# One sixth of the score subtraction through ScalarE and GpSimd, three slot-softmax operations from GpSimd to VectorE, and the row-max selector product in fp32r

## The chip, the cores and the metric

The kernel runs on one core of a Trainium2 chip. The metric is the device time of one execution in microseconds (us); before the change it is 1116.34 us, the median of three runs (1116.29 to 1117.21). Each engine works through its own queue in order: TensorE (PE; its weight loads are listed apart as PEld), VectorE (DVE), ScalarE (ACT), GpSimd (POOL), and SyncE (SP), which issues DMAs.

## The reference

Attention over pooled keys, then a soft mixture of experts on its output:

```python
kv_flat = kv_pool.reshape(B, -1, C) @ w_sr          # 4 batches, 768 keys each, C = 128
k = v = kv_flat
s = scale * (q @ k.transpose(0, 2, 1))               # 12288 queries a batch
a = np.exp(s - s.max(-1, keepdims=True))
a /= a.sum(-1, keepdims=True) + 1e-09
x = (a @ v).reshape(B * S, D)
logits = x @ phi                                     # 32 slots
d = softmax of logits over all rows (axis 0)
slot_input = d.T @ x                                 # 8 experts, 4 slots each
slot_out[e] = np.maximum(slot_input[e] @ w1[e], 0.0) @ w2[e]
return softmax of logits over the slots (axis 1) @ slot_out
```

## The kernel before, in words

The 49152 queries are cut into 96 blocks of 512 (index `i`), the 768 keys of a batch into six tiles of 128. Scores stand transposed in PSUM, keys on the partitions and queries along the row, in three PSUM tiles `s_0`, `s_1`, `s_2` of two key tiles each; each exists once, so the scores of the next block can be written only when those of this block have been read. A block goes through these steps:

- `q_hi` (ACT, L462) and `q_lo` (POOL, L466) split the queries into two parts, and `qk` (PE, L476 to L478) makes three products for each key tile: 18 products of 512 columns.
- The maximum over the keys of each query: `rowmax1` (DVE, L483), a transposing reduction, once for each PSUM tile; `rowmax2` (DVE, L493 and L495); `rowmax_pe` (PE, L503), which multiplies with a constant selector matrix `sel` in fp32; `rowmax3` (DVE, L508); and `rowmax4` (DVE, L513), which writes the maximum over all partitions as `mb`.
- `sub` (DVE, L521) subtracts `mb` from the scores in four instructions: key tiles 0 and 1 together, 2, 3, then 4 and 5 together. Three key tiles make one half, `t_0` or `t_1`.
- For each half: `exp_hi` (ACT, L528) writes the exponential `phi` in fp16, `exp_t` (ACT, L532) the same in fp32, and `plo` (POOL, L537) their difference, 128x1536 elements.
- The products with the values, `av_hi` (PE, L554 and L555) and `av_lo` (PE, L562), are made about two blocks later, and `av_evac` (ACT, L572) copies them out.

Four blocks make a group, which goes through the slot softmax with a running maximum. Its steps that matter here: `g1l` (L626) makes the logits `LL`; `g2` (DVE, L631 and L633) takes their maximum; `g2q`, `g2h`, `g2l`, `g3m`, `g3` (L588, L643, L647, L654, L661 to L668) turn that into the new running maximum `mrun`; `g4` (L673 and L678) subtracts it; `g5e` (ACT, L682) takes the exponential; `g5m` (L688 and L690) weights it; `g7m` (PE, L707) adds up the slot inputs. `k_max` (DVE, L718), `k_sub` (L723) and `k_exp` (ACT, L728) belong to the softmax over the slots. In nearly all groups `g1l`, `g4`, `g5m` and `k_sub` run on GpSimd.

The order of the instructions on PE, DVE, ACT and POOL is not the order of the code. A planner (`Plan`) takes every step with an engine, a cost in us, a latency, a priority and what it depends on, plays the four queues through with these costs, and issues the steps in the order that comes out. A step marked `hot` (the chain from L493 to L513) may hold an engine back for it. So a changed cost or engine of one step moves many others, and what was issued next to what has to be read from the built program. A block gets 9.8 us in its table (`PER`).

Of the kernel before, what the change touches and what calls it, by code (L numbers as in the profile page):

```python
# [172 lines left out]
def attention_then_soft_moe(ctx: ExitStack, tc: tile.TileContext, qT, kv0, kvT, w_sr, w_srT, phi, w1, w2, outT):  # L173
# [71 lines left out]
    nc.vector.tensor_copy(sel_bf, sel)
# [59 lines left out]
    def kv_pool(h, c):  # L305
        w = KS[h][1] - KS[h][0]
        v = kvs[h, c]
        if c == 0:
            kvs[h] = sp.tile([P, TH, BQ], F32, tag="t", name=f"pool_{h}", bufs=TBUF).rearrange("p a b -> p (a b)")
        a = kvs[h][:, : 2 * w]  # L310
        if c == 2:
            nc.vector.tensor_tensor(out=a, in0=kvs[h, 0], in1=v, op=ALU.add)
        elif c:
            nc.vector.tensor_tensor(out=a, in0=a, in1=v, op=ALU.add)
# [174 lines left out]
    def rowmax2(i):  # L489
        top = banks[plan.bank][:, 512 - (NQD + 1) * NBK :]  # L490
        pq = PQ[i] = top[:, NBK:]
        r1 = top[:, :NBK]
        nc.vector.tensor_reduce(out=r1, in_=MX[i].rearrange("p t b -> p b t"), axis=X, op=ALU.max)  # L493
# [1 line left out]
        nc.vector.tensor_tensor(  # L495
            out=rq, in0=r1.unsqueeze(1).broadcast_to([P, NQD, NBK]),
            in1=quad.unsqueeze(2).broadcast_to([P, NQD, NBK]), op=ALU.mult,
        )
        MX[i] = rq

    def rowmax_pe(i):
        pqv = PQ.pop(i)
        nc.tensor.matmul(pqv, sel, MX[i].rearrange("p k b -> p (k b)"), start=True, stop=True)  # L503
# [12 lines left out]
    def sub(i, t, n):  # L516
        h, o = divmod(t, TH)
        if o == 0:
            TT_[i, h] = sp.tile([P, TH, BQ], F32, tag="t", name=f"t_{i}_{h}", bufs=TBUF)
# [1 line left out]
        nc.vector.tensor_tensor(  # L521
            out=TT_[i, h][:, o : o + n, :], in0=S[i, t // 2][:, u : u + n, :],
            in1=MX[i].unsqueeze(1).broadcast_to([P, n, BQ]), op=ALU.subtract,
        )
# [278 lines left out]

    pooled[0] = bp.tile([P, NK], F32, tag="pooled", name="pooled_0", bufs=1)
    loaded = []
    for n, which in enumerate(LOADS):
        dep = [] if n < 2 else [ops["pool", 0, 6 * (n - 1) - 2]]
        loaded.append(op("SP", 0.3, 0, 0, dep, lambda which=which: start_kv(which)))
        for h, e0, cnt in which:
            for c in range(e0, e0 + cnt, 2):  # L810
# [442 lines left out]
```

## Time and profile before

| | us |
|---|---|
| time, median of 3 runs | 1116.34 |
| profiled execution, first to last instruction | 1112.9 |
| PE busy | 1044.9 |
| DVE busy | 984.2 |
| POOL busy | 870.5 |
| ACT busy | 829.4 |

The profiled execution has no separate time beside its span of 1112.9 us; the runs lie 3.4 us above it, which is what stands around the first and the last instruction. The granted TensorE clock was full from 60 us to 1020 us.

How to read the rows: a timeline row has its start in us, its duration in us, the engine, the line, the operation, what it writes and what it reads, the shape, how many instructions are merged, and in brackets how long the engine was idle before it and who ended that. A row of a group has the count, the busy time in us, the mean duration in ns, and the idle time before it. Starts are those of the record; neighbouring instructions of one engine overlap by some 0.05 to 0.1 us. Blocks are counted from 0; blocks 36 to 39 are one group, and its logits are made while blocks 38 and 39 pass.

### The profile page before, as it was taken

The page shows a single profiled execution, that of the slowest core. Times are in us where ns is not written, and L with a number is a line of the kernel's source. Part 1 is how long each engine was busy: PE and PEld are TensorE (multiplying, and loading weights), DVE is VectorE, ACT ScalarE, POOL GpSimd, SP SyncE. Part 2 cuts the span into 40 slices and gives each one's busy share as a digit, 9 for nine tenths or more (in the row PEclk, how much of TensorE's full clock was granted, in tenths as well). Part 3 has the DMA queues.
Part 4 walks back from the last instruction along what each step waited for, and adds up shares of the span by engine and source line. Part 5 has one row for each costly group of instructions (what it writes and reads, how often), then busy time and mean ns, then how long its engine had stood idle before and what let it go on. Part 6 is the DMA issues. An engine that isn't in the chain of part 4 may idle for free.

```text
span 1112.9 us, 24732 instructions
## 1 busy us (share of the span) xinstructions
PE 1044.9 (94%) x10198; PEld 893.6 (80%) x10198; DVE 984.2 (88%) x1493; ACT 829.4 (75%) x1029; POOL 870.5 (78%) x503
## 2 busy tenths in 40 slices
PE   3699999999999999999999999999999999997885
PEld 2588888888888888888888888888888888886343
DVE  7889889899889989899888988989989988997894
ACT  1677778778777878778777788688778777875563
POOL 0679898798899889789899989789889889873440
PEclk9899999999999999999999999999999999999975
DMA  9218301111136310120145310120110110113498
GB/s 351 108 31 177 70 16 39 39 58 39 39 60 150 82 35 6 39 87 10 39 102 108 82 39 1 39 95 2 39 39 1 39 39 2 39 39 114 145 406 357
DMA packets 17407, 89.15 MB, mean 80 GB/s; under 512 B 1680, under 2 KB 3984, under 8 KB 11152
## 3 DMA queue, kind: packets, MB, share of 16 engines
q1 hardware_dynamic: 13408, 69.47, 17.0%
q0 software_dynamic: 3312, 17.70, 8.4%
q8 instruction: 81, 1.33, 0.5%
q10 hardware_dynamic: 576, 0.41, 0.1%
q14 instruction: 30, 0.25, 0.1%
HBM read 58.87 MB, written 25.17 MB: 76 GB/s over the span
## 4 chain that ended last, share of the span: by engine, by line
PE 61%; ACT 18%; DVE 15%; issue 3%; POOL 2%; DMA 1%; SPq 0%; DVEq 0%; ACTq 0%
PE m L562 10%; PE m L554 10%; PE m L555 9%; ACT phi L528 8%; PE s L476 8%; PE s L478 7%; PE s L477 7%; ACT t L532 7%; DVE t L521 4%; PE m L503 3%; DVE r L483 3%; PE m L707 2%; PE po L1138 2%; DVE o L1147 2%; DVE mb L513 1%
## 5 line engine op out<-in xcount | busy, mean ns | idle before, releaser
L537 POOL TENSOR_TENSOR plo<-t,phi 128x1536 f16<-128x1536 f32 x190 | 598.8, 3156 | 128.1 <-ACT t L532 127.3
L528 ACT ACTIVATE phi<-t,lnk 128x1536 f16<-128x1536 f32 x192 | 301.5, 1570 | 118.9 <-DVE t L521 118.7
L483 DVE TRANSPOSE_TENSOR_REDUCE r<-s 128x32 f32<-128x1024 f32 x288 | 348.6, 1233 | 29.3 <-PE s L478 25.7
L554 PE MATMUL m<-vhi,phi 128*128 128x161 f16 x2280 | 354.7, 234 | 2.8 <-DVE acc L713 1.4
L555 PE MATMUL m<-vlo,phi 128*128 128x160 f16 x2280 | 353.8, 233 | 0.0
L521 DVE TENSOR_TENSOR t<-s,mb 128x1024 f32<-128x1024 f32 (+1 forms) x384 | 342.8, 949 | 9.3
L532 ACT ACTIVATE t<-t,lnk 128x1536 f32<-128x1536 f32 x192 | 301.5, 1570 | 3.6
L476 PE MATMUL s<-qhi,khi 128*128 128x512 f32 x576 | 239.9, 417 | 6.1 <-DVE t L521 5.8
L554 PEld LDWEIGHTS <-phi 128*128 128x128 f16 x2304 | 224.3, 98 | 24.3 <-issue 24.3
L555 PEld LDWEIGHTS <-phi 128*128 128x128 f16 x2304 | 225.1, 98 | 5.4 <-issue 3.5
L562 PE MATMUL m<-vhi,plo 128*128 128x161 f16 x2280 | 226.5, 234 | 0.4 <-POOL plo L537 0.4
L478 PE MATMUL s<-qhi,klo 128*128 128x512 f32 x576 | 226.6, 393 | 0.0
L477 PE MATMUL s<-qlo,khi 128*128 128x512 f32 x576 | 226.1, 392 | 0.0
L562 PEld LDWEIGHTS <-plo 128*128 128x128 f16 x2304 | 178.2, 100 | 1.2 <-POOL plo L537 0.6
L466 POOL TENSOR_TENSOR qlo<-q,qhi 128x512 fp32r<-128x512 f32 x96 | 128.6, 1340 | 26.8 <-ACT qhi L462 26.8
L572 ACT ACTIVATE xl<-m 128x322 f32<-128x322 f32 x189 | 81.4, 430 | 84.5 <-PE m L562 83.8
L476 PEld LDWEIGHTS s<-qhi,khi 128*128 128x128 f32 x576 | 109.2, 190 | 32.6 <-issue 7.5
L478 PEld LDWEIGHTS s<-qhi,klo 128*128 128x128 f32 x576 | 108.8, 189 | 24.7 <-DVE klo L356 0.5
L477 PEld LDWEIGHTS s<-qlo,khi 128*128 128x128 f32 x576 | 109.5, 190 | 18.7 <-issue 0.7
L513 DVE STREAM_TRANSPOSE mb<-m 128x512 f32<-128x512 f32 x96 | 68.3, 711 | 3.3
L462 ACT ACTIVATE qhi<-q 128x512 fp32r<-128x512 f32 x96 | 59.1, 616 | 1.5 <-issue 0.8
L508 DVE TENSOR_REDUCE m<-m 128x16 f32<-128x64 f32 x96 | 21.5, 224 | 40.7 <-PE m L503 40.7
(145 smaller groups left out, 860.1 us busy)
## 6 DMA issues: line engine op xcount, KB each, us to landing
q<-qT SPq DMA_DIRECT2D x23, 1024.0 KB, 4.8
outT<-o SPq DMA_DIRECT2D x21, 1024.0 KB, 5.4
kva<-kvT POOLq DMA_DIRECT2D x9, 1536.0 KB, 11.2
kva<-kvT SPq DMA_DIRECT2D x3, 1536.0 KB, 10.5
kv<-kv SPq DMA_DIRECT2D x8, 512.0 KB, 5.6
w<-w SPq DMA_DIRECT2D x2, 1536.0 KB, 6.4
w<-w SPq DMA_DIRECT2D x4, 768.0 KB, 4.4
outT<-o SPq DMA_DIRECT2D x6, 512.0 KB, 4.7
```

What stands on the lines that cost most here:

```text
L466: nc.gpsimd.tensor_tensor(out=lo, in0=q_src(i), in1=hi.bitcast(F32), op=ALU.subtract)
L476: nc.tensor.matmul(s, khi[:, ks], hi, start=True, stop=False)
L477: nc.tensor.matmul(s, khi[:, ks], lo, start=False, stop=False)
L478: nc.tensor.matmul(s, klo[:, ks], hi, start=False, stop=True)
L483: nc.vector.tensor_reduce(out=MX[i][:, 2 * u : 2 * u + 2, :].rearrange("p t b -> p (t b)"), in_=S[i, u].rearrange("p t (b j) -> p (t b) j" ...
L521: nc.vector.tensor_tensor(out=TT_[i, h][:, o : o + n, :], in0=S[i, t // 2][:, u : u + n, :], in1=MX[i].unsqueeze(1).broadcast_to([P, n, BQ ...
L528: nc.scalar.activation(hi, TT_[i, h], AF.Exp, bias=lnk, scale=SCALE)
L532: nc.scalar.activation(t, t, AF.Exp, bias=lnk, scale=SCALE)
L537: eng.tensor_tensor(out=lo, in0=TT_.pop((i, h)), in1=PP[i, h], op=ALU.subtract)
L554: nc.tensor.matmul(px, p, vhi[:, t, :], start=(t == 0), stop=False)
L555: nc.tensor.matmul(px[:, 1:], p, vlo[:, t, :], start=False, stop=False)
L562: nc.tensor.matmul(px, PP[i, t // TH][1][:, t % TH, ks], vhi[:, t, :], start=False, stop=(t == NT - 1))
```

## The change

It has four parts.

1. For blocks 1 to 94, `sub` no longer does key tile 5. ACT copies its scores from PSUM to a new tile `cs` (`copy`), and GpSimd subtracts the maximum (`sub_c`) and writes the last third of `t_1`. So `exp_hi` of the second half waits for DVE and for GpSimd.
2. `g1l`, `g4` and `k_sub` run on DVE for all groups. `g5m` stays on GpSimd, and so does the small `g2l`.
3. The selector product takes `sel_r`, a copy of `sel` in fp32r, and `rq` in fp32r. It is one pass of the matrix instead of two.
4. The pooled keys of batch 0 lie in a buffer of the ring `phi` instead of one of their own, which gives the room for `cs`.

```diff
+    sel_r = cp.tile([P, P], F32R, tag="sel_r", name="sel_r")
+    nc.vector.tensor_copy(sel_r, sel)
...
+            pooled[0] = sp.tile([P, TH, BQ], F16, tag="phi", name="pooled_0", bufs=PB).rearrange("p a b -> p (a b)").bitcast(F32)
...
-        rq = sp.tile([P, NQD, NBK], F32, tag="rq", name=f"rq_{i}")
+        rq = sp.tile([P, NQD, NBK], F32R, tag="rq", name=f"rq_{i}")
...
-        nc.tensor.matmul(pqv, sel, MX[i].rearrange("p k b -> p (k b)"), start=True, stop=True)
+        nc.tensor.matmul(pqv, sel_r, MX[i].rearrange("p k b -> p (k b)"), start=True, stop=True)
...
+    def copy(i):
+        TT_[i, "c"] = sp.tile([P, BQ], F32, tag="cs", name=f"cs_{i}", bufs=1)
+        nc.scalar.activation(TT_[i, "c"], S[i, NU - 1][:, 1, :], AF.Copy)
+
+    def sub_c(i):
+        nc.gpsimd.tensor_tensor(out=TT_[i, 1][:, TH - 1, :], in0=TT_.pop((i, "c")), in1=MX[i], op=ALU.subtract)
...
-        mul(g).tensor_tensor(out=d["L"], in0=XL[g][:, :, C + 1 :], in1=bc(d["ru"], NS), op=ALU.mult)
+        nc.vector.tensor_tensor(out=d["L"], in0=XL[g][:, :, C + 1 :], in1=bc(d["ru"], NS), op=ALU.mult)
...
-        mul(g).tensor_tensor(
+        nc.vector.tensor_tensor(
             out=d["D"], in0=d["L"], in1=MRUN[g].unsqueeze(1).broadcast_to([P, nt(g), NS]), op=ALU.subtract
         )
...
-            mul(g).tensor_tensor(out=d["da"], in0=MRUN[g - 1], in1=MRUN[g], op=ALU.subtract)
+            nc.vector.tensor_tensor(out=d["da"], in0=MRUN[g - 1], in1=MRUN[g], op=ALU.subtract)
...
-        nc.gpsimd.tensor_tensor(out=c, in0=c, in1=bc(RM[:, o : o + n], NS), op=ALU.subtract)
+        nc.vector.tensor_tensor(out=c, in0=c, in1=bc(RM[:, o : o + n], NS), op=ALU.subtract)
...
+        two = 0 < i < NB - 1
...
-        for t, n in ((0, 2), (2, 1), (3, 1), (4, 2)):
+        for t, n in ((0, 2), (2, 1), (3, 1), (4, 1 if two else 2)):
```

The costs and dependences in the planner's table follow: a cost of 0.16 instead of 0.27 for the selector product, 1.05 for `sub_c`, and DVE costs for the three moved steps.

Three places show what that does to the queues. In the rows the lines are those of each kernel's own file: L487 to L525 of the changed kernel are L483 to L521 of the one before, L535 is `sub_c`, L548 is `plo` (L537 before), L637 to L734 are L626 to L723 before. A number in `r_38` or `m_38` is that of the block; other numbers only keep buffers apart.

VectorE from the last steps of the row maximum of block 38 to the first reduction of block 39, before:

```order
L493 TENSOR_REDUCE m_114<-r_38_5423 128x16
L495 TENSOR_TENSOR rq_5479<-m_114,quad 128x64
L508 TENSOR_REDUCE m_38_5492<-m_114 128x16
L513 STREAM_TRANSPOSE mb_5494<-m_38_5492 128x512
L521 TENSOR_TENSOR t_0_5515<-s_0_5406,mb_5494 128x1024
L521 TENSOR_TENSOR t_0_5515<-s_1_5418,mb_5494 128x512
L521 TENSOR_TENSOR t_1_5542<-s_1_5418,mb_5494 128x512
L521 TENSOR_TENSOR t_1_5542<-s_2_5429,mb_5494 128x1024
L631 TENSOR_REDUCE cm_5560<-LL 128x16
L633 TENSOR_REDUCE cmt_5562<-cm_5560 128x1
L483 TENSOR_REDUCE r_39_5568<-s_0_5544 128x32
```

The same place after the change:

```order
L497 TENSOR_REDUCE m_117<-r_38_5536 128x16
L499 TENSOR_TENSOR rq_5458<-m_117,quad 128x64
L637 TENSOR_TENSOR LL<-xl_5040,ru_5576 128x512
L512 TENSOR_REDUCE m_38_5604<-m_117 128x16
L517 STREAM_TRANSPOSE mb_5608<-m_38_5604 128x512
L642 TENSOR_REDUCE cm_5627<-LL 128x16
L644 TENSOR_REDUCE cmt_5629<-cm_5627 128x1
L525 TENSOR_TENSOR t_0_5652<-s_0_5518,mb_5608 128x1024
L525 TENSOR_TENSOR t_0_5652<-s_1_5531,mb_5608 128x512
L525 TENSOR_TENSOR t_1_5671<-s_1_5531,mb_5608 128x512
L525 TENSOR_TENSOR t_1_5671<-s_2_5542,mb_5608 128x512
L487 TENSOR_REDUCE r_39_5683<-s_0_5665 128x32
```

The logits (`g1l`) now stand between the two halves of the hot chain, in front of `rowmax3`; their reductions stand in front of the subtractions instead of behind them; and the last subtraction has 512 columns instead of 1024.

VectorE one block later, from the last subtraction of block 39 to the maximum of block 40, before:

```order
L521 TENSOR_TENSOR t_1_5691<-s_2_5570,mb_5637 128x1024
L483 TENSOR_REDUCE r_40_5708<-s_0_5687 128x32
L483 TENSOR_REDUCE r_40_5708<-s_1_5704 128x32
L483 TENSOR_REDUCE r_40_5708<-s_2_5715 128x32
L493 TENSOR_REDUCE m_114<-r_40_5708 128x16
L495 TENSOR_TENSOR rq_5764<-m_114,quad 128x64
L508 TENSOR_REDUCE m_40_5776<-m_114 128x16
L513 STREAM_TRANSPOSE mb_5778<-m_40_5776 128x512
```

The same place after the change:

```order
L525 TENSOR_TENSOR t_1_5809<-s_2_5691,mb_5754 128x512
L684 TENSOR_TENSOR D_5822<-LL,mrun_5796 128x512
L689 TENSOR_TENSOR da_5824<-mrun_5216,mrun_5796 128x32
L487 TENSOR_REDUCE r_40_5830<-s_0_5805 128x32
L487 TENSOR_REDUCE r_40_5830<-s_1_5818 128x32
L487 TENSOR_REDUCE r_40_5830<-s_2_5833 128x32
L497 TENSOR_REDUCE m_117<-r_40_5830 128x16
L499 TENSOR_TENSOR rq_5879<-m_117,quad 128x64
L734 TENSOR_TENSOR LL<-LL,RM 128x512
L512 TENSOR_REDUCE m_40_5892<-m_117 128x16
L517 STREAM_TRANSPOSE mb_5896<-m_40_5892 128x512
```

The two instructions of `g4` now stand in front of the reductions of block 40, and `k_sub` in front of its `rowmax3`. `g1l` stands in front of `rowmax3` in 23 groups, `k_sub` in 19, and `g4` behind the last subtraction in 22.

GpSimd around the second half of block 38, before:

```order
L537 TENSOR_TENSOR plo_1_5633<-t_1_5542,phi_1_5582 128x1536
L466 TENSOR_TENSOR qlo_5625<-q_4855,qhi_5624 128x512
L673 TENSOR_TENSOR D_5700<-LL,mrun_5677 128x512
L678 TENSOR_TENSOR da_5702<-mrun_5110,mrun_5677 128x32
L723 TENSOR_TENSOR LL<-LL,RM 128x512
L537 TENSOR_TENSOR plo_0_5725<-t_0_5652,phi_0_5694 128x1536
L688 TENSOR_TENSOR D_5700<-D_5700,rv_5489 128x512
L690 TENSOR_TENSOR da_5702<-da_5702,sel_102 128x32
L537 TENSOR_TENSOR plo_1_5802<-t_1_5691,phi_1_5739 128x1536
```

After the change, where `plo_0_5702` is the first half of block 38 and `plo_0_5843` that of block 39:

```order
L548 TENSOR_TENSOR plo_0_5702<-t_0_5652,phi_0_5673 128x1536
L470 TENSOR_TENSOR qlo_5724<-q_4948,qhi_5723 128x512
L548 TENSOR_TENSOR plo_1_5779<-t_1_5671,phi_1_5700 128x1536
L535 TENSOR_TENSOR t_1_5809<-cs_5752,mb_5754 128x512
L548 TENSOR_TENSOR plo_0_5843<-t_0_5769,phi_0_5812 128x1536
L699 TENSOR_TENSOR D_5822<-D_5822,rv_5624 128x512
L701 TENSOR_TENSOR da_5824<-da_5824,sel_102 128x32
L548 TENSOR_TENSOR plo_1_5922<-t_1_5809,phi_1_5857 128x1536
```

The three `g4` and `k_sub` instructions (L673, L678, L723) are gone from here, and `sub_c` of block 39 stands directly behind the second `plo` of block 38.

More of the change, by code (lines that the diff above doesn't have):

```diff
@@ L275, in attention_then_soft_moe @@
         "m": 2, "t": TBUF, "phi": PB, "plo": PB, "q": 2, "qs": 2, "xl": 2, "D": 1, "kv": 2,
-        "pooled": 1, "v32": 1, "r6": 2, "rq": 2, "m1": 2, "mb": 1, **{f"s{u}": 1 for u in range(NU)},
+        "cs": 1, "v32": 1, "r6": 2, "rq": 2, "m1": 2, "mb": 1, **{f"s{u}": 1 for u in range(NU)},
     })
@@ L307, in kv_pool @@
         v = kvs[h, c]
+        if c == 0 and h == 0:
+            pooled[0] = sp.tile([P, TH, BQ], F16, tag="phi", name="pooled_0", bufs=PB).rearrange("p a b -> p (a b)").bitcast(F32)
         if c == 0:
@@ L802, in pw_out @@
         nc.scalar.activation(w_sb[:, C:], PK_.pop("w")[:, :NS], AF.Copy)
-    pooled[0] = bp.tile([P, NK], F32, tag="pooled", name="pooled_0", bufs=1)
     loaded = []
@@ L814, in attention_then_soft_moe @@
                     [loaded[-1]] + ([ops["pool", h, c - 2]] if c else []), lambda h=h, c=c: kv_pool(h, c), at=lands[h, c],
-                    acq=[("t", ("pool", h))] if c == 0 else [], use=[("t", ("pool", h))] if c else [],
+                    acq=([("phi", "pooled")] if h == 0 else []) + [("t", ("pool", h))] if c == 0 else [],
+                    use=([("t", ("pool", h))] if c else []) + ([("phi", "pooled")] if c or h else []),
                 )
@@ L822, in kv_ops @@
     def kv_ops(b, base, step, dep0, dep1):
-        kvu = [("kv", b)] if b else []
+        kvu = [("kv", b)] if b else [("phi", "pooled")]
         at_ = {}
@@ L888, in group_ops @@
         go("1u", small, sm_(1), [o["0r"]], g1u)
-        go("1l", big, bg(), [o["1u"]], g1l)
+        go("1l", "DVE", dve(n512), [o["1u"]], g1l)
         go("1v", small, sm_(2), [o["0r"]], g1v)
@@ L900, in group_ops @@
         ops["g3", g] = o["3"]
-        go("4", big, bg(1.3) + 0.25, [o["3"]], g4, acq=[("D", g)])
+        go("4", "DVE", dve(n512) + 0.1, [o["3"]], g4, acq=[("D", g)])
         go("5e", "ACT", act(n512) + 0.13, [o["4"]], g5e, use=[("D", g)])
@@ L964, in attention_then_soft_moe @@
             t0 = t
-        se = {0: ops["s", i, 2], 1: ops["s", i, 4]}
+        se = {0: [ops["s", i, 2]], 1: [ops["s", i, 4]]}
+        if two:
+            se[1].append(op(
+                "POOL", 1.05, 0.1, T0 - 6, [c_, r4, ops["s", i, 3]], lambda i=i: sub_c(i),
+                use=[("cs", i), ("mb", i), ("t", (i, 1))],
+            ))
         for h in range(NH):
-            e1 = op("ACT", act(TH * BQ, 1), 0.1, T0 + 6 + 3.2 * h, [se[h]], lambda i=i, h=h: exp_hi(i, h), acq=[("phi", (i, h))], use=[("t", (i, h))])
+            e1 = op("ACT", act(TH * BQ, 1), 0.1, T0 + 6 + 3.2 * h, se[h], lambda i=i, h=h: exp_hi(i, h), acq=[("phi", (i, h))], use=[("t", (i, h))])
             e2 = op("ACT", act(TH * BQ, 1), 0.1, T0 + 7.6 + 3.2 * h, [e1], lambda i=i, h=h: exp_t(i, h), use=[("t", (i, h))], raw=0.13)
@@ L1024, in attention_then_soft_moe @@
         a = op("DVE", dve(n), 0.08, p, [ops["L", g]] + late, lambda g=g: k_max(g))
-        a = op("POOL", 1.05 * n / 512, 0.1, p, [a, ops["g4", g]], lambda g=g: k_sub(g))
+        a = op("DVE", dve(n), 0.08, p, [a, ops["g4", g]], lambda g=g: k_sub(g))
         ops["ke", g] = op("ACT", act(n), 0.1, p, [a], lambda g=g: k_exp(g))
```

7 lines of the change are left out of this document (6 added, 1 removed).

## Prediction

> **What bounds the kernel now.** I read the page first (busy times, the chain that ended last), then the busy time of one group of blocks, then the timelines of VectorE and GpSimd in it.
>
> ```profile
> PE 1044.9 (94%) x10198; PEld 893.6 (80%) x10198; DVE 984.2 (88%) x1493; ACT 829.4 (75%) x1029; POOL 870.5 (78%) x503
> PE 61%; ACT 18%; DVE 15%; issue 3%; POOL 2%; DMA 1%; SPq 0%; DVEq 0%; ACTq 0%
> 395.50:435.90 40.40, 39.87 (x404) 35.12 (x403) 36.57 (x54) 31.87 (x39) 34.74 (x20) 1.00 0.08 28
> ```
>
> The third row is one group of four blocks, 40.40 us. TensorE is busy for 39.87 of it, which would be the whole story if the others followed it freely; but matmul ends are modelled, and VectorE with 36.57 us hangs in one loop with TensorE: scores, reductions, selector product, maximum, subtraction, next scores. Blocks 38 and 39 on VectorE show the loop:
>
> ```profile
> 418.97 0.22 DVE L495 TENSOR_TENSOR rq<-m,quad 128x64 f32<-128x64 f32 x1
> 419.78 0.22 DVE L508 TENSOR_REDUCE m<-m 128x16 f32<-128x64 f32 x1 [0.59 <-PE m L503]
> 420.04 0.71 DVE L513 STREAM_TRANSPOSE mb<-m 128x512 f32<-128x512 f32 x1
> 420.86 3.55 DVE L521 TENSOR_TENSOR t<-s,mb 128x1024 f32<-128x1024 f32 x4
> 424.32 0.70 DVE L631 TRANSPOSE_TENSOR_REDUCE cm<-LL 128x16 f32<-128x512 f32 x1
> 425.14 2.37 DVE L483 TRANSPOSE_TENSOR_REDUCE r<-s 128x32 f32<-128x1024 f32 x2
> ...
> 429.11 0.23 DVE L495 TENSOR_TENSOR rq<-m,quad 128x64 f32<-128x64 f32 x1
> 429.25 0.68 DVE L718 TENSOR_REDUCE RM<-LL 128x16 f32<-128x512 f32 x1
> 429.93 0.23 DVE L508 TENSOR_REDUCE m<-m 128x16 f32<-128x64 f32 x1
> 430.19 0.71 DVE L513 STREAM_TRANSPOSE mb<-m 128x512 f32<-128x512 f32 x1
> 431.00 1.22 DVE L521 TENSOR_TENSOR t<-s,mb 128x1024 f32<-128x1024 f32 x1
> 432.69 2.41 DVE L521 TENSOR_TENSOR t<-s,mb 128x512 f32<-128x512 f32 x3
> 435.02 3.50 DVE L483 TRANSPOSE_TENSOR_REDUCE r<-s 128x32 f32<-128x1024 f32 x3
> 438.62 0.33 DVE L493 TENSOR_REDUCE m<-r 128x16 f32<-128x96 f32 x1
> 438.99 0.23 DVE L495 TENSOR_TENSOR rq<-m,quad 128x64 f32<-128x64 f32 x1
> 439.80 0.22 DVE L508 TENSOR_REDUCE m<-m 128x16 f32<-128x64 f32 x1 [0.59 <-PE m L503]
> 440.06 0.71 DVE L513 STREAM_TRANSPOSE mb<-m 128x512 f32<-128x512 f32 x1
> ```
>
> From one maximum (L513) to the next VectorE idles only the 0.59 us in which it waits for the selector product. So in these two blocks VectorE's queue sets the pace as much as TensorE does. How much delay TensorE forgives is read from the first product of the next scores, in the same round:
>
> ```profile
> L476 PE MATMUL s<-qhi,khi x1: 477/477/477, 422.6 to 422.6; 128*128 128x512 f32 x1
> ```
>
> It starts at 422.6; the subtraction that frees its PSUM tile ends at 420.86 + 1.22 = 422.08. The slack is 0.5 us.
>
> **The change part by part.** The prices of the single operations, from the groups kept apart by shape:
>
> ```profile
> L521 DVE TENSOR_TENSOR t<-s,mb 128x1024 f32<-128x1024 f32 x192 | 233.9, 1218 | 9.3
> L466 POOL TENSOR_TENSOR qlo<-q,qhi 128x512 fp32r<-128x512 f32 x96 | 128.6, 1340 | 26.8 <-ACT qhi L462 26.8
> L521 DVE TENSOR_TENSOR t<-s,mb 128x512 f32<-128x512 f32 x192 | 122.9, 680 | 0.0
> L503 PE MATMUL m<-rq,sel 128*128 128x64 f32 x192 | 39.8, 289 | 12.7 <-ACT t L532 6.7 <-DVE rq L495 3.9
> L1122 ACT ACTIVATE chi<-m 128x512 fp32r<-128x512 f32 x23 | 13.6, 594 | 6.0 <-PE m L1116 6.0
> L314 DVE TENSOR_TENSOR pool<-pool,kv 128x512 f32<-128x512 f32 x6 | 4.1, 690 | 0.2
> ```
>
> *Selector product.* The two fp32 passes take 39.8 / 96 = 0.415 us a block, one pass 0.289, so one pass instead of two saves 0.13 us. No row shows an fp32r product of 64 columns: it cannot save more than half of 0.415 (0.21), and a pass as long as today's two would save nothing. I take 0.13, from the row of one pass.
>
> *Copy and `sub_c`.* The last subtraction becomes 1218 - 680 = 0.54 us shorter on VectorE. ACT gets 94 copies of about 0.59 us (L1122 also reads 128x512 from PSUM); it stands at 75% and the copy comes before `mb` is known, so this costs nothing unless ACT is late by more. GpSimd gets 94 subtractions of 1.34 us (L466, two full inputs). The Trainium skill, GPSIMD Engine Reference, section "3.1 Elementwise — side-by-side cycle accounting", gives about 2.6 cycles an element at 1.2 GHz, which would make it 1.11 us; by that the sum below would be some 0.23 x 22 = 5 us lower. The row decides.
>
> *Moved operations.* A subtraction of this size on VectorE is 0.69 us from SBUF (L314; 0.61 to the next start). Three a group and the small `da` are some 2.2 us, the four shorter subtractions return 2.16: VectorE's sum stays what it was. None of them issues a DMA. What counts is where they stand, and whom they meet. Two rows of VectorE and one of GpSimd at the start of the kernel:
>
> ```profile
> 9.43 0.22 DVE L241 COPY sel<-sel 128x128 f32<-128x128 f32 x1
> 9.56 1.22 DVE L314 TENSOR_TENSOR pool<-pool,kv 128x1024 f32<-128x1024 f32 x1
> 10.70 1.29 DVE L245 CAST sel_bf<-sel 128x128 bf16<-128x128 f32 x1
> 10.49 1.41 POOL L466 TENSOR_TENSOR qlo<-q,qhi 128x512 fp32r<-128x512 f32 x1 [8.96 <-ACT qhi L462]
> ```
>
> A copy of 128 columns takes 0.22 us, but the cast of the same size, started while GpSimd subtracted, took 1.29 and ended at 11.99, right behind GpSimd's end at 11.90. And GpSimd's instruction, which met the two-input L314, is 0.07 us longer than its group's mean. So a VectorE operation between SBUF tiles waits until GpSimd's running instruction is over. The subtractions from PSUM show nothing of the kind: their rows stay at 0.68 and 1.22 beside a GpSimd that works 78% of the time. I take it that the three moved operations, which read both inputs from SBUF, wait as the cast did; bounds are no wait at all, and a whole `plo` of 3.1 us each time. The Trainium skill, SBUF — State Buffer, section "Who interferes with whom", says the same: VectorE with two SBUF inputs contends with a GpSimd instruction that reads SBUF, and the second to issue blocks until the first has finished. By that rule the forecast below holds; the trace shows the cast's wait of 1.07 us, not one of a two-input operation.
>
> Where GpSimd stands then:
>
> ```profile
> 416.56 3.12 POOL L537 TENSOR_TENSOR plo<-t,phi 128x1536 f16<-128x1536 f32 x1 [3.00 <-ACT t L532]
> ...
> 423.72 1.32 POOL L466 TENSOR_TENSOR qlo<-q,qhi 128x512 fp32r<-128x512 f32 x1
> 426.16 3.11 POOL L537 TENSOR_TENSOR plo<-t,phi 128x1536 f16<-128x1536 f32 x1 [1.12 <-ACT t L532]
> ...
> 436.74 3.12 POOL L537 TENSOR_TENSOR plo<-t,phi 128x1536 f16<-128x1536 f32 x1 [0.43 <-ACT t L532]
> 439.81 1.06 POOL L688 TENSOR_TENSOR D<-D,rv 128x512 f32<-128x512 f32 x1
> ```
>
> Now the group, from maximum to maximum:
>
> - *To block 38: +0.51.* `g1l` comes to VectorE at 419.19, when L495 ends; `plo` runs until 419.68. A wait of 0.49 and 0.61 of work put L508 1.10 us behind L495's end instead of 0.59. The shorter product is lost in that. `g2` in front of the subtractions (0.82, from 424.32 to 425.14) makes the first one 1.33 late against a slack of 0.5: TensorE idles some 0.8 us here.
> - *To block 39: -0.07.* The reductions are VectorE-bound: 0.54 saved, L718 (0.61) now among them, the gap with L718 in it (0.82) back to 0.81 - 0.13.
> - *To block 40: +1.38, and 0.31 with `k_sub`.* Before, 9.87 us (430.19 to 440.06) without a free moment but the product. The last subtraction ends 0.54 earlier, 4.3 us after the maximum began. GpSimd: `plo` of block 38 starts 6.12 after its maximum began (426.16 - 420.04), with `g2` in front and one ACT step less between it is about 6.8; `plo`, `qlo`, `plo` are 7.5 more, 14.3, and that is 4.2 after the maximum of block 39 began, 10.1 later. So `g4` arrives just when `sub_c` (1.34) begins or is queued, and its first or its second instruction sits through it: 1.3 us of wait and 0.75 of work, minus 0.54, minus 0.13 for the product. `k_sub` then comes 10.5 after the maximum, when L688 ends (439.81 + 1.06 - 430.19 = 10.68): 0.17 of wait and 0.61 of work against the 0.46 that the product leaves free, 0.31.
> - *To block 41: -0.4.* TensorE-bound: 0.13 for the product, and 0.3 because TensorE has done its value products when the late maximum comes, and starts the scores 2.25 instead of 2.56 after it.
>
> Sum: 0.51 x 23 - 0.07 x 22 + 1.38 x 22 + 0.31 x 19 - 0.4 x 22 = 37.6 us, by the counts in the built program. At the start the cast of `sel_r` adds 0.2; at the end `k_sub` of the last groups stands in front of work that the rest waits for, 0.6. The pooled keys' other place costs nothing, for the buffers of `phi` are used for the first time after it. Together 38 us; the sum is made on the profiled execution of 1112.9 us and put on the median of 1116.3: **1155 us**. What `sub_c` makes the second exponential wait for lies inside: in block 40 it ends some 4 us after the maximum, and ACT asks for it at 6.
>
> **The rivals.** *No wait (a faster kernel).* If two-input operations do not wait for GpSimd, or meet it idle, the same steps are: to 38 +0.04 (0.61 in a gap of 0.59), to 39 -0.07, to 40 +0.08 (1.38 - 1.3) and 0.15 for `k_sub`, to 41 -0.4: about -0.2 a group, 5 us, 1112 us. With 0.21 for the product, 0.08 more in each block that TensorE bounds, two a group: 1108. It decides from 0.2 us of wait a group downwards. For it: only a cast shows the wait in this trace. Against it: GpSimd is busy in 34.74 of 40.40 us now, and after the change in 34.7 - 3.5 + 5.4 = 36.6, so there is little idle time to meet.
>
> *GpSimd wins the races.* Behind each instruction of GpSimd stands the next. If VectorE, which has waited, does not get its turn, `g1l` sits through the second `plo` too: 3.1 us a group more, 23 x 3.1 = 71 us, 1226. Against it: that `plo` needs an exponential which ends at about the same time as the first, so GpSimd has nothing ready at that moment.
>
> *GpSimd becomes the bound.* Of a group's 42 us it has 36.6 of work and some 2 in which VectorE holds it up. If `sub_c` slips past the moment at which ACT asks for it, by more than its 2 us of margin, each us more is one in the loop of the block: with 1 us in one block of four, 22 us more, 1177.
>
> **How the numbers follow.** Chances: forecast 0.60, no wait 0.23, GpSimd as the bound 0.10, lost races 0.07. A measurement tells apart about 0.2%, 2 us, here 1114 to 1118.5. Of the no-wait case 0.19 lies below that; the rest of it and a tenth of the forecast (waits that nearly cancel) are within: 0.19 faster, 0.09 same, 0.72 slower. The forecast's own range takes the wait of `g4` from 0 to a whole `plo` (1155 - 29 to 1155 + 40, 1126 to 1195). The range reaches down to the no-wait time with the better product, 1108, and up to 1190; some 0.2 is left out.
>
> **What would show it.** Right: the rows of `g1l`, `g4` and `k_sub` on VectorE have means well above 0.69 us (about 1.1, 1.3 and up, 0.9), their ends fall together with ends of GpSimd's rows, TensorE's idle time before the scores grows, and a group takes 42 us. The product's group is at about half its 39.8 us or a little more. Wrong: these rows at 0.69 us; then the time is near 1112, or the loss lies elsewhere. `plo` or `sub_c` longer by 0.6 us would show the wait on the other side. Wrong too, if ACT's rows before L528 name GpSimd: then the third rival is the cause.

## The result and the profile after

The changed kernel takes **1173.93 us** (median of 4 runs, 1173.38 to 1174.13) where the kernel before takes 1116.32 (4 runs, 1115.95 to 1117.21): 1.0508 times as long, with an interval of 1.0496 to 1.0521. The profiled execution has a span of 1172.4 us, 59.5 more than before. The medians differ by 57.6: in the runs that have both figures, the time lies 1.7 to 1.9 us above the span. So the 3.4 us that was said of the kernel before is not all time around the first and the last instruction; its profiled execution seems to have been a shorter one than the median.

The page's busy times and the shares of the chain that ended last:

```profile
PE 1051.9 (90%) x10102; PEld 893.4 (76%) x10102; DVE 1034.7 (88%) x1587; ACT 880.1 (75%) x1123; POOL 920.1 (78%) x504
PE 55%; DVE 37%; ACT 4%; issue 3%; DMA 1%; POOL 0%; DVEq 0%; SPq 0%; ACTq 0%
```

VectorE's share of the chain that ended last went from 15% to 37%, TensorE's fell from 61% to 55%. VectorE's busy time grew by 50.5 us, though the operations it gained and lost were about equal. The groups by shape show where that sits (count, busy us, mean ns, idle time before them):

```profile
L637 DVE TENSOR_TENSOR LL<-xl,ru 128x512 f32<-128x512 f32 x23 | 42.1, 1829 | 0.0
L684 DVE TENSOR_TENSOR D<-LL,mrun 128x512 f32<-128x512 f32 x23 | 32.4, 1409 | 0.0
L734 DVE TENSOR_TENSOR LL<-LL,RM 128x512 f32<-128x512 f32 x23 | 25.0, 1088 | 0.0
L525 DVE TENSOR_TENSOR t<-s,mb 128x512 f32<-128x512 f32 x286 | 179.2, 681 | 0.0
L535 POOL TENSOR_TENSOR t<-cs,mb 128x512 f32<-128x512 f32 x94 | 122.7, 1306 | 3.3 <-DVE mb L517 3.3
L507 PE MATMUL m<-rq,sel_r 128*128 128x64 f32 x96 | 26.7, 278 | 28.8 <-DVE rq L499 23.1 <-ACT t L543 3.3
```

`g1l`, `g4` and `k_sub` do as much work as a subtraction of 512 columns, which takes 0.68 us when it reads PSUM (L525). Their rows are 1.6 to 2.7 times as long, and no idle time stands before them: the wait lies inside the instruction, and the profile counts it as busy.

The timelines of VectorE and GpSimd from block 38 to 40 (start, duration):

```profile
439.46 0.22 DVE L499 TENSOR_TENSOR rq<-m,quad 128x64 fp32r<-128x64 f32 x1
439.60 1.08 DVE L637 TENSOR_TENSOR LL<-xl,ru 128x512 f32<-128x512 f32 x1
440.60 0.21 DVE L512 TENSOR_REDUCE m<-m 128x16 f32<-128x64 f32 x1
440.92 0.71 DVE L517 STREAM_TRANSPOSE mb<-m 128x512 f32<-128x512 f32 x1
...
450.96 0.71 DVE L517 STREAM_TRANSPOSE mb<-m 128x512 f32<-128x512 f32 x1
...
455.19 1.49 DVE L684 TENSOR_TENSOR D<-LL,mrun 128x512 f32<-128x512 f32 x1
456.61 0.18 DVE L689 TENSOR_TENSOR da<-mrun,mrun 128x32 f32<-128x32 f32 x1
...
460.68 0.22 DVE L499 TENSOR_TENSOR rq<-m,quad 128x64 fp32r<-128x64 f32 x1
460.82 1.23 DVE L734 TENSOR_TENSOR LL<-LL,RM 128x512 f32<-128x512 f32 x1
461.98 0.21 DVE L512 TENSOR_REDUCE m<-m 128x16 f32<-128x64 f32 x1
```

```profile
437.01 3.12 POOL L548 TENSOR_TENSOR plo<-t,phi 128x1536 f16<-128x1536 f32 x1 [1.64 <-ACT t L543]
440.41 3.23 POOL L548 TENSOR_TENSOR plo<-t,phi 128x1536 f16<-128x1536 f32 x1 [0.28 <-ACT t L543]
...
454.85 1.29 POOL L535 TENSOR_TENSOR t<-cs,mb 128x512 f32<-128x512 f32 x1
457.39 3.11 POOL L548 TENSOR_TENSOR plo<-t,phi 128x1536 f16<-128x1536 f32 x1 [1.25 <-ACT t L543]
460.46 1.05 POOL L699 TENSOR_TENSOR D<-D,rv 128x512 f32<-128x512 f32 x1
461.46 0.70 POOL L701 TENSOR_TENSOR da<-da,sel 128x32 f32<-128x32 f32 x1
```

Read them side by side. `g1l` starts at 439.60; `plo` ends at 437.01 + 3.12 = 440.13, and `g1l` ends 0.55 us later, at 440.68. `g4` starts at 455.19; `sub_c` ends at 454.85 + 1.29 = 456.14, and `g4` ends 0.54 later. `k_sub` starts at 460.82; `g5m` (L699) ends at 461.51, and `k_sub` ends 0.54 later. Each time VectorE waits for GpSimd's running instruction and then needs 0.55 us. The wait works the other way too: the small L701 (128x32), queued while `k_sub` ran, takes 0.70 us and ends 0.1 us after it.

The busy times of this group of four blocks (span, then PE, PEld, DVE, ACT and POOL), and the waits of TensorE for VectorE over the whole span (us in total, times, longest), after the change and before it:

```profile
420.28:462.29 42.01, 39.87 (x399) 34.65 (x399) 38.20 (x57) 34.11 (x44) 36.84 (x19) 1.00 0.08 27
```

```profile
PE m L565 <- DVE m L512: 34.7, 43, 5.3
PE m L507 <- DVE rq L499: 23.1, 24, 2.0
```

```profile
PE m L554 <- DVE m L508: 1.3, 3, 0.7
PE m L503 <- DVE rq L495: 3.9, 9, 2.0
```

A group took 40.4 us and takes 42.0 now. TensorE's two waits sum to 57.8 us and were 5.2 before, so they grew by 52.6 us, most of the 59.5. The first is that of the value products for `rowmax3` (L512), in front of which `g1l` or `k_sub` stands; the second that of the selector product for L499, which `g4` has pushed back.

### The profile page after: what moved, and what is told of

Read it like the earlier page. It is cut to its first block, busy times and chain, and to the rows that moved or that the text cites. A ratio compares the mean times of both kernels' runs of the same rounds, so it can differ in the third digit from the quotient of the medians.

```text
span 1172.4 us, 24753 instructions
## 1 busy us (share of the span) xinstructions
PE 1051.9 (90%) x10102; PEld 893.4 (76%) x10102; DVE 1034.7 (88%) x1587; ACT 880.1 (75%) x1123; POOL 920.1 (78%) x504
## 4 chain that ended last, share of the span: by engine, by line
PE 55%; DVE 37%; ACT 4%; issue 3%; DMA 1%; POOL 0%; DVEq 0%; SPq 0%; ACTq 0%
DVE r L487 13%; PE m L565 9%; PE m L566 8%; PE m L573 8%; PE s L480 8%; PE s L481 7%; PE s L482 7%; DVE t L525 4%; DVE LL L637 3%; DVE D L684 2%; PE m L718 2%; DVE LL L734 2%; DVE mb L517 2%; DVE m L497 1%; PE po L1160 1%
## 5 line engine op out<-in xcount | busy, mean ns | idle before, releaser
L548 POOL TENSOR_TENSOR plo<-t,phi 128x1536 f16<-128x1536 f32 x190 | 597.1, 3147 | 133.0 <-ACT t L543 123.4
L565 PE MATMUL m<-vhi,phi 128*128 128x161 f16 x2280 | 361.4, 236 | 35.0 <-DVE m L512 34.7
L487 DVE TRANSPOSE_TENSOR_REDUCE r<-s 128x32 f32<-128x1024 f32 x288 | 351.6, 1237 | 38.7 <-PE s L482 30.5
L566 PE MATMUL m<-vlo,phi 128*128 128x160 f16 x2280 | 360.5, 235 | 0.0
L525 DVE TENSOR_TENSOR t<-s,mb 128x512 f32<-128x512 f32 (+1 forms) x384 | 292.5, 819 | 2.5
L566 PEld LDWEIGHTS <-phi 128*128 128x128 f16 x2304 | 227.9, 99 | 41.3 <-issue 40.7
L565 PEld LDWEIGHTS <-phi 128*128 128x128 f16 x2304 | 226.8, 99 | 23.8 <-issue 23.8
L573 PE MATMUL m<-vhi,plo 128*128 128x161 f16 x2280 | 230.6, 236 | 0.0
L573 PEld LDWEIGHTS <-plo 128*128 128x128 f16 x2304 | 172.5, 99 | 0.8 <-issue 0.7
L470 POOL TENSOR_TENSOR qlo<-q,qhi 128x512 fp32r<-128x512 f32 x96 | 126.2, 1315 | 26.3 <-ACT qhi L466 26.3
L535 POOL TENSOR_TENSOR t<-cs,mb 128x512 f32<-128x512 f32 x94 | 122.7, 1306 | 3.3 <-DVE mb L517 3.3
L517 DVE STREAM_TRANSPOSE mb<-m 128x512 f32<-128x512 f32 x96 | 68.3, 712 | 10.0
L758 POOL TENSOR_TENSOR LL<-LL,RM 128x512 f32<-128x512 f32 (+2 forms) x25 | 24.8, 1015 | 57.7 <-DVE RM L753 57.7
```

Source lines behind the costliest of these rows:

```text
L470: nc.gpsimd.tensor_tensor(out=lo, in0=q_src(i), in1=hi.bitcast(F32), op=ALU.subtract)
L487: nc.vector.tensor_reduce(out=MX[i][:, 2 * u : 2 * u + 2, :].rearrange("p t b -> p (t b)"), in_=S[i, u].rearrange("p t (b j) -> p (t b) j" ...
L525: nc.vector.tensor_tensor(out=TT_[i, h][:, o : o + n, :], in0=S[i, t // 2][:, u : u + n, :], in1=MX[i].unsqueeze(1).broadcast_to([P, n, BQ ...
L548: eng.tensor_tensor(out=lo, in0=TT_.pop((i, h)), in1=PP[i, h], op=ALU.subtract)
L565: nc.tensor.matmul(px, p, vhi[:, t, :], start=(t == 0), stop=False)
L566: nc.tensor.matmul(px[:, 1:], p, vlo[:, t, :], start=False, stop=False)
```

## The experiments

The theory is that of the forecast: a VectorE operation with two SBUF inputs waits until GpSimd's running instruction is over. Every ratio below is to runs of the kernel before that were made beside it (medians 1116.0 to 1116.2 us). The main rival is that the places of the three operations in VectorE's queue cost the time, whatever they wait for.

**One input instead of two** (`one_input`). The same order on every engine; only the kind of the three operations changes.

```diff
-        nc.vector.tensor_tensor(out=d["L"], in0=XL[g][:, :, C + 1 :], in1=bc(d["ru"], NS), op=ALU.mult)
+        nc.vector.tensor_reduce(out=d["L"], in_=XL[g][:, :, C + 1 :].unsqueeze(3), axis=X, op=ALU.max)
...
+        nc.vector.tensor_reduce(out=d["D"], in_=d["L"].unsqueeze(3), axis=X, op=ALU.max)
...
+        nc.vector.tensor_reduce(out=c, in_=c.unsqueeze(3), axis=X, op=ALU.max)
```

> The changed kernel with the same instructions in the same order, but the three moved operations (logits, subtraction of the running maximum with its small da, subtraction of the row maximum) are reductions over an axis of one element: one SBUF input, the same sizes, the same places. Left out is what these operations compute (scaling and subtractions; the exponentials behind them get a tiny scale so that they stay finite). Theory 1 (the moved operations wait for GpSimd's running instruction, in the hot chain): their rows, now 1.83, 1.41 and 1.09 us in the mean, fall to about 0.68; the waits sum to some 55 us (42.1 + 32.4 + 25.0 + 7.2 less 23 times three of 0.69 and 24 of 0.18), part of it in gaps, so the time falls from 1174 to 1112 to 1130. Theory 2 (the places in the queue cost it, or GpSimd and ACT with the new copy and subtraction): rows may fall, the time stays above 1155.

It took 1108.4 us (1107.91 to 1109.53), 0.9931 of before (0.9917 to 0.9946), some 4 us below the range of the first theory. The three groups:

```profile
L637 DVE TENSOR_REDUCE LL<-xl 128x512 f32<-128x512 f32 x23 | 15.5, 676 | 0.0
...
L684 DVE TENSOR_REDUCE D<-LL 128x512 f32<-128x512 f32 x23 | 15.6, 677 | 0.0
...
L732 DVE TENSOR_REDUCE LL<-LL 128x512 f32<-128x512 f32 x23 | 15.6, 677 | 0.0
```

At the same places, beside the same GpSimd, operations of the same size take 0.68 us, and the time falls by 65.5 us, the whole loss and 8 us more. So the places by themselves do not cost it. The edit also changes the kind of operation, from `tensor_tensor` to a reduction; but the subtractions of L525 are `tensor_tensor` too, with one input in PSUM, and take 0.681 us. What costs is the second SBUF input. The converse, that one SBUF input is always safe, is not shown: the cast in the prediction's rows has one input and waited 1.07 us.

**The moves alone, and all but the moves** (`moves_only`, `no_moves`). The first is the kernel before with the three operations on VectorE; the second the changed kernel with them on GpSimd. Here the planner makes new orders.

```diff
-        mul(g).tensor_tensor(out=d["L"], in0=XL[g][:, :, C + 1 :], in1=bc(d["ru"], NS), op=ALU.mult)
+        nc.vector.tensor_tensor(out=d["L"], in0=XL[g][:, :, C + 1 :], in1=bc(d["ru"], NS), op=ALU.mult)
```

> The kernel before with the three operations moved to VectorE and nothing else of the change: no copy, no GpSimd subtraction, selector product in fp32. Theory 1: the logits and the row-maximum subtraction again stand in front of rowmax3, the other behind the last score subtraction, and wait there; GpSimd has 5.4 us a group less to do than in the changed kernel, so the waits are a little shorter, but VectorE has 0.54 us a block more: 1150 to 1185. Theory 2 (copy and GpSimd subtraction cost it): 1110 to 1130.

> The changed kernel with the three operations back on GpSimd: copy, GpSimd subtraction and fp32r product stay. GpSimd then has some 40 us of work in a group of 40.4. Theory 1: no two-input operation of VectorE is left in the loop, so the loss is gone; 1100 to 1130, where the upper end is GpSimd as the bound. Theory 2: above 1150.

`moves_only` took 1180.28 us (1179.66 to 1185.7), 1.0585 (1.0559 to 1.061); `no_moves` 1108.35 (1105.56 to 1109.29), 0.9925 (0.9909 to 0.9942). So the moves lose about 65 us with the other parts (1173.93 - 1108.35) and 64 without them. The groups of `moves_only` show that the same operations wait elsewhere when they meet other instructions:

```profile
L724 DVE TENSOR_TENSOR LL<-LL,RM 128x512 f32<-128x512 f32 x23 | 38.0, 1651 | 0.0
L627 DVE TENSOR_TENSOR LL<-xl,ru 128x512 f32<-128x512 f32 x23 | 37.0, 1609 | 0.0
...
L674 DVE TENSOR_TENSOR D<-LL,mrun 128x512 f32<-128x512 f32 x23 | 18.5, 805 | 0.0
```

Without `sub_c`, `g4` waits 0.1 us on average instead of 0.7, but `k_sub` 1.0 instead of 0.4.

**The product alone** (`product_only`): the kernel before with the selector product in fp32r.

```diff
-        nc.tensor.matmul(pqv, sel, MX[i].rearrange("p k b -> p (k b)"), start=True, stop=True)
+        nc.tensor.matmul(pqv, sel_r, MX[i].rearrange("p k b -> p (k b)"), start=True, stop=True)
```

> The kernel before with the fp32r selector product alone. Both theories: one pass instead of two saves 0.13 us a block on TensorE and the same in VectorE's gap (0.59 to 0.46): up to 12 us, 1104 to 1114. If the fp32r pass were as long as two fp32 passes: 1116.

1103.5 us (1103.13 to 1103.74), 0.9885 (0.9869 to 0.9902): the fastest version, ahead of both kernels and 0.5 us below the range that was expected. Its group:

```profile
L505 PE MATMUL m<-rq,sel_r 128*128 128x64 f32 x96 | 26.9, 280 | 13.0 <-ACT t L534 6.6 <-DVE rq L497 4.3 <-ACT qhi L464 0.2
```

One pass of 0.28 us instead of two that took 0.415; 96 times 0.135 is 13 us, and 12.6 arrive. `no_moves` adds `copy`, `sub_c` and the other place of the pooled keys to that and is 4.9 us slower, so these parts don't pay either. Why they cost 4.9 us was not taken apart.

**One operation at a time** (`g1l_one`, `g4_one`, `ksub_one`). The first experiment's edit for one operation each; the order stays.

```diff
-        nc.vector.tensor_tensor(out=c, in0=c, in1=bc(RM[:, o : o + n], NS), op=ALU.subtract)
+        nc.vector.tensor_reduce(out=c, in_=c.unsqueeze(3), axis=X, op=ALU.max)
```

> The changed kernel with its order on every engine kept; of the three moved operations only g1l is a one-input reduction over an axis of one (it leaves out the scaling of the logits, and the exponentials get a scale of 1e-12, which changes no duration). In the changed kernel's trace g1l's rows last 26 us longer than the one-input rows of the same size, g4's 16.5, da's 3, k_sub's 9, together 54.7 us, for a loss of 65.5 us. Theory (each two-input operation waits for GpSimd's running instruction, and the loss goes with the waits): g1l gives back 26.2 / 54.7 x 65.5 = 31 us: 1143 us (1137 to 1149), and the groups of 47 and 48 us are gone, since the five rows of 3 to 6 us were all g1l's. Rival (a wait removed moves the other two operations into a worse meeting with GpSimd): under 20 us are given back, above 1154. Rival (the place in the chain, not the wait): within 3 us of 1174.

> The same with g4 and its small da alone as one-input reductions (leaves out the subtraction of the running maximum). Theory: (16.5 + 2.9) / 54.7 x 65.5 = 23 us given back: 1151 us (1145 to 1157). Rival (worse meetings of the others): above 1160. Rival (place): within 3 us of 1174.

> The same with k_sub alone as a one-input reduction (leaves out its subtraction of the row maximum). Theory: 9.1 / 54.7 x 65.5 = 11 us given back: 1163 us (1158 to 1168). The three savings add up to 65 us if the waits do not act on each other; a sum under 50 would mean that they do. Rival (place): within 3 us of 1174.

| one input in | us | ratio to before | given back | by the waits |
|---|---|---|---|---|
| `g1l` | 1142.0 (1140.85 to 1143.28) | 1.023 (1.0213 to 1.0247) | 31.9 | 31 |
| `g4`, `da` | 1149.91 (1149.28 to 1150.47) | 1.0299 (1.0281 to 1.0317) | 24.0 | 23 |
| `k_sub` | 1162.9 (1162.1 to 1163.84) | 1.0417 (1.0401 to 1.0434) | 11.0 | 11 |

The sum is 66.9 us against 65.5 for all three together: the waits add up. The rows lasted 54.7 us longer than one-input rows, so each us of waiting in them costs 1.2 us of time.

**A probe of the wait by itself** (`probe`), a program of its own with GpSimd's and VectorE's operations alone.

```diff
+    def plo():
+        nc.gpsimd.tensor_tensor(out=lo, in0=big, in1=half, op=ALU.subtract)
+    def spacer():
+        nc.vector.tensor_tensor(out=three, in0=s, in1=small, op=ALU.subtract)
+    def two_in():
+        nc.vector.tensor_tensor(out=two, in0=small, in1=wide[:, :512], op=ALU.subtract)
+    def one_in():
+        nc.vector.tensor_reduce(out=one, in_=small.unsqueeze(2), axis=X, op=ALU.max)
```

> No attention at all: four stages in which GpSimd makes 24 subtractions of plo's size (128x1536, every one ready) and VectorE 22 operations of 128x512, with one to four subtractions from PSUM between two of them. Stage 1, VectorE's operations read two SBUF tensors: theory, each waits for the end of the running plo, rows between 0.7 and 3.8 us, mean about 2, none above 3.8 (it gets its turn at the next end), and the plo behind it is about 0.6 us longer; the subtractions from PSUM stay at 0.68. Rival (GpSimd, having its next instruction ready, keeps the turn): rows of 4 us and more already here. Stage 2, one-input operations: 0.68 us each. Stage 3, as stage 1, with three transfers that GpSimd issues (1536 KB each, accumulating) in flight: if these are what makes VectorE lose its turn, as in blocks 30 and 54 of the changed kernel, rows above 3.8 us here, some 4 to 7, and none in stage 1. Stage 4, as stage 1, with three transfers of the same size that SyncE issues: as stage 1, if it is GpSimd's transfers; as stage 3, if it is any traffic.

The groups of all stages together, two inputs from SBUF (L44), one from PSUM (L41), one input (L47):

```profile
L41 DVE TENSOR_TENSOR three<-s,small 128x512 f32<-128x512 f32 x220 | 151.0, 686 | 4.5
L44 DVE TENSOR_TENSOR two<-small,wide 128x512 f32<-128x512 f32 x66 | 131.2, 1988 | 0.0
L47 DVE TENSOR_REDUCE one<-small 128x512 f32<-128x512 f32 x22 | 14.8, 675 | 0.0
```

```profile
L44 DVE TENSOR_TENSOR two<-small,wide x66: 681/2255/3482, 16.2 to 330.3; 128x512 f32<-128x512 f32 x66
```

Of these three kinds only the one with two SBUF inputs waits. No row exceeds 3.48 us, so VectorE got its turn at the end of the running instruction every time, although GpSimd had its next one ready. A `plo` behind such an operation takes 3.42 us instead of 3.09, 0.33 longer where 0.6 was expected, by the rows of `plo` in stage 2 and in stage 4 (shortest, median, longest in ns, first and last start):

```profile
L38 POOL TENSOR_TENSOR lo<-big,half x23: 3088/3095/3106, 93.5 to 163.3; 128x1536 f16<-128x1536 f32 x23
L38 POOL TENSOR_TENSOR lo<-big,half x23: 3087/3422/3427, 255.4 to 332.1; 128x1536 f16<-128x1536 f32 x23
```

The transfers were to tell apart what makes VectorE lose its turn; in no stage did it lose it, so the rows above 3.8 us that were expected in stage 3 did not come. SyncE's transfers did not keep to stage 4 (the output's ran during stage 1, the three others in stage 3, none in stage 4), so only the absence of a loss can be read, not a comparison of GpSimd's transfers with SyncE's.

**The transfer ahead of the lost turns** (`acc_fill`, `acc_later`). Two rows of `g1l` are far longer than one `plo`. GpSimd and VectorE in block 30 of the changed kernel:

```profile
346.18 1.20 POOL L329 DMA_DIRECT2D kva<-kvT  x1
346.96 6.61 POOL L548 TENSOR_TENSOR plo<-t,phi 128x1536 f16<-128x1536 f32 x2
353.12 1.66 POOL L470 TENSOR_TENSOR qlo<-q,qhi 128x512 fp32r<-128x512 f32 x1
...
349.27 6.07 DVE L637 TENSOR_TENSOR LL<-xl,ru 128x512 f32<-128x512 f32 x1
```

Here, behind the issue of a transfer (L329), GpSimd's queue runs ahead: `plo` starts 0.42 us before the issue ends (347.38), `qlo` 0.45 before the second `plo` ends (353.57). `g1l` sits through all three and ends at 355.34, 0.56 after `qlo`. Block 54 shows the same, 6.05 us; `g4_one` (6.08 and 6.09) and `ksub_one` (6.00 and 6.13) repeat it, and in `moves_only` there is one such row of 5.88 us, again behind the issue of a transfer. The experiments move that issue behind `qlo` at these two places and put an operation without a transfer there, or nothing.

```diff
-            nc.gpsimd.dma_start(out=kvs[b], in_=kvT[b - 1, :, c * KVC : (c + 1) * KVC, :], accum_op=ALU.add, ...)
+            go = lambda: nc.gpsimd.dma_start(...)
+            if b > 1 and c == 2:
+                LATER.append(go)          # issued by q_lo, behind its subtraction
+                nc.gpsimd.tensor_tensor(out=scr, in0=..., in1=..., op=ALU.subtract)   # acc_fill only
```

> The changed kernel with the same order on every engine but GpSimd, and there with one difference at two places (blocks 30 and 54): the accumulating transfer that GpSimd issues directly ahead of the two plo and qlo (1.2 us of issuing) goes behind them, and an operation of about the same length without a transfer (128x512, from a constant) stands in its place. So the two plo run when they ran, and g1l meets the first of them at the same moment. Theory: it is the issue of the transfer that makes GpSimd start each following instruction 0.45 us before the end of the one before, and so keep the turn; without it g1l waits for the end of the running plo only: its two rows of 6.05 and 6.07 us become some 1.7 us, their groups 43 to 44 us instead of 48.2, and the time 1164 to 1166 us instead of 1173.9. Rival (g1l loses because the second plo is ready in time, whoever stood ahead): the rows stay at 6 us and the time within 2 us of 1174.

> The same without the operation in its place: the two plo begin up to 1.2 us earlier, as soon as their exponential is there. Theory: g1l meets the end of the first plo or the moment between the two; its two rows become 0.7 to 1.7 us and the time 1163 to 1166 us. Rival (the second plo is ready in time and keeps the turn, whatever stood ahead): rows of 4 us and more, within 4 us of 1174.

`acc_fill` took 1163.63 us (1163.35 to 1163.73), 1.0424 (1.0407 to 1.0442); `acc_later` 1163.32 (1161.41 to 1164.43), 1.0421 (1.0405 to 1.0436): the first 0.4 us below its expected range, the second within. The same place in `acc_fill`:

```profile
345.93 1.04 POOL L338 TENSOR_TENSOR scr<-quad 128x512 f16<-128x512 f32 x1
346.93 6.63 POOL L560 TENSOR_TENSOR plo<-t,phi 128x1536 f16<-128x1536 f32 x2
353.51 1.30 POOL L481 TENSOR_TENSOR qlo<-q,qhi 128x512 fp32r<-128x512 f32 x1
...
348.96 1.62 DVE L649 TENSOR_TENSOR LL<-xl,ru 128x512 f32<-128x512 f32 x1
```

The two `plo` run when they ran, `g1l` comes while the first is running as it did, and now it gets its turn at that one's end: 1.62 us, and 1.64 in block 54. Moving the issue returns 10.3 us. Its transfer moves along with it, so the kernel does not tell the two apart; in the probe, transfers in flight made no row longer than 3.48 us.

What in the run-ahead costs VectorE its turn stays open. In the probe, which also issued such transfers, the `plo` behind the issue started 0.41 us early too, but the one after it did not. In the kernel the second `plo` also waits for an exponential of ScalarE; a probe with such a wait was not tried. And the run-ahead alone is not enough. In `acc_fill` the issue of the next transfer stands ahead of a `plo` in block 32, and `k_sub` (L746 there) meets the queue that runs ahead:

```profile
367.55 3.55 POOL L560 TENSOR_TENSOR plo<-t,phi 128x1536 f16<-128x1536 f32 x1
370.62 1.48 POOL L711 TENSOR_TENSOR D<-D,rv 128x512 f32<-128x512 f32 x1
371.63 1.13 POOL L713 TENSOR_TENSOR da<-da,sel 128x32 f32<-128x32 f32 x1
...
370.73 1.93 DVE L746 TENSOR_TENSOR LL<-LL,RM 128x512 f32<-128x512 f32 x1
```

`k_sub` sits through L711, which had started 0.11 us before it, and ends 0.56 us after that one's end (372.10). The small L713 had started 0.47 us before this end, and yet it did not go first. The same happens once more in `acc_fill` (1.77 us) and twice in `acc_later` (2.02 and 1.84).

## Why the prediction was right, and where it was off

The forecast's mechanism, two-input operations of VectorE that wait for GpSimd in front of the chain, held at each place it named. Its size was a third short (38 us forecast, 57.6 measured), and some of its terms were wrong in ways that cancel. The one row it had for the wait, a cast, reads a single input, and the reductions with a single input did not wait. So that the cast and the moved operations wait for the same cause was taken, not shown; the second input was the right condition.

The table compares the time from one maximum to the next, worked out from the starts of the `mb` rows (L513 before, L517 after), as the mean of the four groups from block 73 to block 88.

| interval | before | after | measured | forecast |
|---|---|---|---|---|
| to block 38 (`g1l`, `g2`) | 9.62 | 9.96 | +0.34 | +0.51 |
| to block 39 | 10.14 | 10.03 | -0.11 | -0.07 |
| to block 40 (`g4`, `k_sub`) | 9.88 | 11.33 | +1.45 | +1.69 |
| to block 41 | 10.79 | 10.68 | -0.11 | -0.4 |
| group | 40.44 | 41.99 | +1.55 | +1.73 |

- **`g1l`.** In such a group it waits 0.53 us (forecast 0.49). The delay of the block is smaller than forecast: behind the wait `rowmax3` starts 0.47 us after `plo`'s end (440.13 to 440.60), not 0.61. That 0.61 was given with L314, whose rows of this size have their next start 0.71 us later or more. And TensorE does not lose it where the forecast put it, before the scores: it stands before the value products, at L565, until `rowmax3` has come.
- **`g4` behind `sub_c`.** It sits through `sub_c`, as said, with a mean row of 1.41 us against 1.3 and up, and `k_sub` has 1.09 against 0.9. But the sum counted a wait of 1.3 us for `g4` and 0.17 for `k_sub`; in these four groups their rows are 1.51 and 1.21 us, which are waits of 0.83 and 0.53 beside 0.68 of work. The two misses nearly cancel, so that +1.45 lies close to +1.69 is partly luck.
- **To block 41.** The 0.3 us that TensorE was to make good did not come; only the product's share did.
- **Product.** 0.137 us a block (0.415 - 0.278), forecast 0.13; `product_only` confirms that it arrives.
- **`sub_c` and `copy`.** 1.306 and 0.584 us, forecast 1.34 and 0.59. By an estimate from the figure of the Trainium skill (GPSIMD Engine Reference, section "3.1 Elementwise — side-by-side cycle accounting") `sub_c` would take 1.11 us; the trace's row decides against it.
- **Covers.** GpSimd's work in a group is 36.84 us, forecast 36.6, and ScalarE has no wait for `sub_c` in the trace: GpSimd as the bound falls. The no-wait rival gave 1112, and 1108 with a product that saves 0.21 us; `one_input` takes 1108.4, but with a product that saves 0.137. So its price was some 4 us too high, and its condition is not met.
- **Chances.** They were added up a little off: the parts that the forecast names make 0.10 for the same time and 0.71 for slower, not 0.09 and 0.72.
- **The mis-sized term is `g1l` times 23.** The sum gave each of the 23 groups the same 0.49 us of wait. Five did not have it: in blocks 22, 46 and 70 `plo` had just begun, and the rows took 3.29, 3.50 and 3.47 us; in blocks 30 and 54 GpSimd kept the turn, 6.07 and 6.05. These five are 16.9 us longer than at 1.10 each, and one `da` near the end takes 3.07 instead of 0.18. That is 19.8 us of rows, close to the 18.9 that the forecast lacked, but the time went otherwise: from maximum to maximum, these five groups grew by some 32 us in all, 24 more than five usual ones, and the other seventeen from block 5 to block 92 by 1.47 each, less than the 1.73 of the forecast. `g1l_one` takes all of `g1l`'s waits away and returns 31.9 us, `acc_fill` the two lost turns alone, 10.3; the three waits for a whole `plo` were not tried by themselves.
- **The lost turns.** They were a rival, with GpSimd having "nothing ready at that moment" against it. That holds in the usual groups, where the second `plo` starts 0.28 us after the first ends, when its exponential is there. But it is not what decides: in `acc_fill` the second `plo` of block 30 is ready in time (the two take 6.63 us without a gap) and VectorE goes first. In all seven rows of a lost turn, in four kernels, GpSimd's queue ran ahead behind the issue of a transfer, which the forecast did not reckon with. Since `k_sub` got its turn against such a queue four times, what decides is not fully known.

The Trainium skill, SBUF — State Buffer, section "Who interferes with whom", says that a VectorE instruction with two SBUF inputs contends with a GpSimd instruction that reads SBUF, and that the pair of ports which the two share is an exclusive lock. `one_input` and the probe agree (0.68 us with one input, 1.99 on average with two). In blocks 30 and 54 two instructions of GpSimd that started after `g1l` went ahead of it; the section does not say when that happens.

## What to carry to other kernels

Before moving an elementwise operation from a busy GpSimd to VectorE, look at its operands: with both in SBUF it is not priced at its 0.68 us but at the rest of whatever GpSimd is running and 0.55 us of work. Here that made rows of up to 3.5 us, in a few places 6, and each us of waiting in a chain which TensorE follows cost 1.2 us. A wait of this kind shows as a longer row with no idle time before it, so compare the mean of a row with one of the same size from PSUM, and look at its longest rows too: the five longest of `g1l`'s 23 rows made some 24 us of the 57.6 here. Parts of a change should be timed alone: here the product alone gained 12.6 us, which the moves' loss of 65 us had hidden.

## What the runs showed of the hardware beyond that

- Behind the issue of a GpSimd transfer, GpSimd's next instructions can start 0.3 to 0.5 us before the one ahead ends. In seven rows a VectorE operation with two SBUF inputs then sat through three of them (5.88 to 6.13 us, where about 1.6 was enough without the issue); in four other rows (1.77 to 2.02 us) it got its turn all the same.
- One-input reductions of 128x512 in SBUF take 0.676 us beside a working GpSimd, and 0.675 in the probe: no wait at all. A cast of 128x128 in SBUF, with one input too, took 1.29 us beside GpSimd in the kernel before, and 0.22 in the changed one.
- A selector product of 64 columns takes 0.278 us in fp32r; in fp32 its two passes took 0.415.
